# Token-major k of batch 0 by TensorE transposes, weights in 4 KB rows, two loads of constants and a first table laid anew

## The chip, the cores and the metric

One core of a Trainium2 chip runs the kernel. The metric is the device time of one execution in microseconds, lower is better. Three executions of the kernel before took 506.74, 506.96 and 507.01 us; the median, 506.96 us, is the time that counts.

## The reference, cut to what is computed

```python
def _attn_ref(q, k, v):                       # q, k, v: (8, 8, 576, 64): batch, head, position, feature
    scores = np.matmul(q, k.transpose(0, 1, 3, 2)) / np.sqrt(64)
    gamma = 1.0 - 2.0 ** (-5.0 - np.arange(8))
    rel = pos[:, None] - pos[None, :]
    Dmat = np.where(rel >= 0, gamma[:, None, None] ** rel, 0.0)
    return np.matmul(scores * Dmat, v)        # retention: causal, decaying with distance

def _moe_ref(x, w_in, w_spatial, b_spatial, w_out):   # x: (8, 576, 512), the heads side by side
    h = np.maximum(x @ w_in, 0.0)             # w_in 512 x 1024, float64
    u, v = h[..., :512], h[..., 512:]
    v_n = (v - v.mean(-1)) / np.sqrt(v.var(-1) + 1e-06)
    v_s = np.einsum('ts,bsd->btd', w_spatial, v_n) + b_spatial[None, :, None]
    return (u * v_s) @ w_out                  # w_out 512 x 512, float64
```

## The kernel before, in words

**Tiling.** Each of the 8 batches goes through a retention stage and then a gated stage. The 576 positions are four chunks of 128 and a tail of 64. Per chunk, retention needs q and k feature-major (`qk`, 128 partitions x 1024), v token-major (`vv`) and k token-major, scaled by a decay per head (`kn`). In the kernel before, `kn` is a second load of k from HBM, and `prep_k` scales it in place.

**Weights.** `w_in` and `w_out` arrive as 64-bit floats. `weight(kind, i)` turns one block into two fp32r parts, a high and a low one, in six steps over DVE, ACT, DVE, DVE, ACT and one more engine. Kind 1 is the v half of `w_in` (blocks of 128 rows, staged in `lent_slot`, parts in `win`), kind 0 its u half and kind 2 `w_out` (blocks of 128 columns, staged in `raw`). With the parts each product is three matmuls: high by high, high by low, low by high. Where matmuls of 512 columns write `m<-win,slot`, that is x times the v half; three of them are one group here.

**What sets the order.** Everything is written out by hand in tables of words. `run` walks a table and lets the named generator issue its next step, so each engine gets its instructions in the table's order and never passes one that waits. `ORDER` holds batches 0 and 1 whole and the retention of batch 2; `STEADY` follows four times and `LAST` ends it. `BANKS` names the PSUM bank of each product in turn. The words that matter here:

- `d.b.c` issues a load of chunk c of batch b on SP (SyncE's DMA queue); `D.kind.i` a block of weights; `c.a`, `c.t` constants; `T` a tail; `S` a part of `w_spatial`.
- `k.b.c` is `prep_k`, `q.b.c` is `prep_q` (q times a decay, tile `qsc`, on POOL).
- `g.b.c`: the scores of a chunk (`r<-qk`), then their mask on DVE (`at`).
- `p.b.c`: the update, k token-major times v (`r<-vv,kn`), then `sh`, decay, `st`, decay: the running state, on DVE and ACT (`dec`).
- `b.b.c`: the burst that ends a chunk: half of the carried products (`r<-qsc,sh`), a one-column copy on ACT (`r<-warm`), the other half, the values (`r<-at,vv`), and two evacuations, `slot` high on ACT and `slot` low on DVE.
- `v.b.s`: x times the v half for chunk s (4 the tail), then its norm. `t`, `e`: the tail. `U`, `V`, `G`, `P`, `y`, `X`, `F`: the later products of batches 0 and 1.
- `z.i.1`: one matmul of zeros, 128 x 512 (`m<-wsp`), that nobody reads. The table has 43 of them.

An instruction is named in the profile by the line of the helper that records it, L203, so the tiles tell them apart. Chunks of batch 0 wait in four places: chunks 0 and 1 in `qk`, `kn`, `vv`, chunk 2 in the tile `u`, chunk 3 in `lent_wout`.

## Time and profile before

| | |
|---|---|
| median of 3 executions | 506.96 us |
| the profiled execution | 506.91 us, of which the span from the first to the last instruction is 504.8 us |
| PE (TensorE matmul) busy | 498.3 us, 99% of the span |
| DVE, ACT, POOL busy | 389.2, 259.2, 152.5 us |
| DMA | 55.52 MB, 110 GB/s over the span |
| chain that ended last | PE 92%, DVE 4%, DMA 3%, ACT 1% |

Busy time of PE is modelled from its pipelined matmuls and says little where every slice is full; what a matmul takes is better read as the distance from one start to the next. The first 22 us are the only stretch in which the chain that ended last runs through DMA, ACT and DVE and not through PE.

### The profile page before, as it was taken

How to read it: one execution, taken by the hardware profiler on the slowest of the kernel's cores; microseconds unless marked ns; L12 is line 12 of the kernel's file. 1: busy time of each engine (PE TensorE's matmuls, PEld its weight loads, DVE VectorE, ACT ScalarE, POOL GpSimd, SP SyncE). 2: the span in 40 equal slices, each digit the busy share in tenths (PEclk: the TensorE clock that was granted, in tenths of full speed). 3: DMA queues.
4: the chain of work that ended last, by engine and by line, in shares of the span. 5: the costliest groups of instructions: out<-in, count | busy, mean ns of one | idle time of the engine just before them, and what ended most of it. 6: DMA issues, size and time to landing. Idle time of an engine off the chain costs nothing.

```text
span 504.8 us, 17011 instructions
## 1 busy us (share of the span) xinstructions
PE 498.3 (99%) x7335; PEld 472.8 (94%) x7335; DVE 389.2 (77%) x869; ACT 259.2 (51%) x587; POOL 152.5 (30%) x133
## 2 busy tenths in 40 slices
PE   8999999999999999999999999999999999999997
PEld 6688999999999999999999999999999999999997
DVE  3787798875899876888679786888867886788756
ACT  3788535654363642647236472446525574357513
POOL 1778733252137421335014250243303240020000
PEclk9999999999999999999999999999999999999999
DMA  8979340332426322153122442054221520011002
GB/s 283 410 260 316 113 142 3 96 112 95 121 65 189 127 66 84 57 176 94 63 79 92 150 141 80 6 162 148 72 86 41 186 91 3 1 36 59 1 2 94
DMA packets 29516, 55.52 MB, mean 110 GB/s; under 512 B 2945, under 2 KB 15361, under 8 KB 29186
## 3 DMA queue, kind: packets, MB, share of 16 engines
q1 hardware_dynamic: 29442, 54.45, 32.6%
q8 instruction: 57, 0.93, 0.8%
q14 instruction: 17, 0.14, 0.1%
HBM read 45.00 MB, written 9.44 MB: 108 GB/s over the span
## 4 chain that ended last, share of the span: by engine, by line
PE 92%; DVE 4%; DMA 3%; ACT 1%; issue 0%; SPq 0%
PE m L203 78%; PE r L203 13%; DVE u L203 2%; DMA lent_slot<-in_w_in 2%; DMA fixed_terms<-in_terms 1%; DVE slot L203 1%; ACT slot L203 1%; DVE lent_vn L203 0%; DVE m L203 0%; SPq L203 0%; DVE st L203 0%; DVE at L203 0%
## 5 line engine op out<-in xcount | busy, mean ns | idle before, releaser
L203 PE MATMUL m<-wsp,vn 128*128 128x288 f32 x768 | 113.8, 297 | 0.0
L203 PEld LDWEIGHTS m<-wsp,vn 128*128 128x128 f32 x768 | 105.7, 188 | 0.7
L203 DVE TENSOR_TENSOR u<-m,u 128x288 f32<-128x288 f32 (+1 forms) x132 | 57.2, 438 | 17.2 <-PE m L203 9.8
L203 ACT COPY u<-m 128x288 f32<-128x288 f32 (+1 forms) x92 | 34.6, 384 | 33.2 <-PE m L203 24.4
L203 PE MATMUL m<-slot,win 128*128 128x288 f32 x336 | 50.5, 296 | 0.0
L203 PEld LDWEIGHTS m<-slot,win 128*128 128x128 f32 x336 | 46.7, 188 | 0.8 <-ACT u L203 0.2
L203 DVE SCALAR_TENSOR_TENSOR u<-u,m 128x288 f32<-128x288 f32 x48 | 21.2, 451 | 25.3 <-PE m L203 25.1
L203 PE MATMUL m<-slot,wout 128*128 128x288 f32 x264 | 39.8, 296 | 0.0
L203 POOL TENSOR_TENSOR slot<-u,slot 128x576 fp32r<-128x576 f32 x7 | 10.0, 1432 | 93.2 <-ACT slot L203 93.2
L203 PEld LDWEIGHTS m<-slot,wout 128*128 128x128 f32 x264 | 36.5, 188 | 0.6 <-DVE vn L203 0.3
L203 PE MATMUL m<-win,slot 128*128 128x512 f32 (+1 forms) x168 | 37.0, 351 | 0.0
L203 ACT CAST slot<-u 128x576 fp32r<-128x576 f32 x32 | 21.5, 675 | 25.6 <-DVE u L203 25.4
L203 PEld LDWEIGHTS m<-win,slot 128*128 128x128 f32 x168 | 26.7, 188 | 4.7 <-DVE slot L203 0.4
L203 ACT CAST places<-u 128x576 fp32r<-128x576 f32 x21 | 14.2, 677 | 30.5 <-DVE u L203 30.3
L203 PE MATMUL m<-quarter,slot 128*128 128x256 f32 x216 | 29.7, 283 | 0.0
L203 ACT COPY r<-warm 1x2 f32<-1x2 f32 x32 | 4.9, 152 | 47.8 <-PE r L203 47.6
L203 DVE TENSOR_TENSOR at<-r,fixed_terms 128x512 f32<-128x512 f32 x32 | 21.9, 683 | 8.5 <-PE r L203 6.9
L203 POOL TENSOR_TENSOR kn<-kn,fixed_terms 128x512 f32<-128x512 f32 x15 | 16.1, 1075 | 39.3 <-DMA kn<-in_qkv 34.1
L203 POOL TENSOR_TENSOR places<-x,places 128x576 fp32r<-128x576 f32 x6 | 10.5, 1756 | 57.0 <-ACT places L203 55.3
L203 PE MATMUL m<-slot,part 128*128 128x288 f32 x168 | 27.3, 301 | 0.4
L203 PE MATMUL m<-wtl,vt 128*128 128x288 f32 (+1 forms) x128 | 27.4, 295 | 0.0
L203 PEld LDWEIGHTS m<-quarter,slot 128*128 128x128 f32 x216 | 26.9, 188 | 0.4
(164 smaller groups left out, 1214.4 us busy)
## 6 DMA issues: line engine op xcount, KB each, us to landing
qk<-in_qkv SPq DMA_DIRECT2D x30, 512.0 KB, 4.3
kn<-in_qkv SPq DMA_DIRECT2D x30, 256.0 KB, 4.8
vv<-in_qkv SPq DMA_DIRECT2D x30, 256.0 KB, 4.7
out<-u SPq DMA_DIRECT2D x28, 144.0 KB, 1.8
tail<-in_tails SPq DMA_DIRECT2D x8, 384.0 KB, 3.5
out<-o SPq DMA_DIRECT2D x18, 144.0 KB, 1.9
lent_slot<-in_w_in SPq DMA_DIRECT2D x4, 512.0 KB, 9.3
raw<-in_w_in SPq DMA_DIRECT2D x4, 512.0 KB, 11.2
```

The lines of the kernel that those rows point to most:

```text
L203: ins = op(*args, **kw)
```

## The change

Token-major k of the four chunks of batch 0 is no longer loaded. `prep_k` makes it with four TensorE transposes per chunk, from feature-major k and an identity (`eye`, 64 KB, a new load), into a PSUM bank, and the scaling then reads that bank and writes `kn`. `k.0.c` is therefore two steps in the table. In HBM the order of v and k token-major is exchanged, so that chunks 2 and 3 are one load of three quarters. The constants are cut in two: `fixed_terms` without the decay of q, and `qs`. The host lays the blocks of the u half and of `w_out` out so that each partition reads one row of 4 KB. The tail of `w_spatial` is stored twice, for one load where there were two. `ORDER` and `BANKS` are new throughout; `STEADY` and `LAST` are as before.

```diff
 ORDER = """
-    d.0.0 d.0.0 c.a q.0.0.p d.0.0 z.22.1 k.0.0.v z.4.1 z.0.1 z.12.1 z.26.1 z.36.1 z.27.1 z.17.1 z.18.1 z.29.1
...
+    d.0.0 z.32.1 z.5.1 z.12.1 z.21.1 c.e d.0.0 c.a z.29.1 z.25.1 z.31.1 z.8.1 z.6.1 z.10.1 z.4.1 z.28.1 z.18.1
...
-    fixed_terms = cp.tile([P, 2 * NP * D + NP * D + H + NP], F32, name="fixed_terms")
+    fixed_terms = cp.tile([P, 2 * NP * D + H + NP], F32, name="fixed_terms")
...
+    qs = cp.tile([P, NP, D], F32, name="qs")
...
+    def eye():
+        return keep("eye", [P, P], tag="o1")
...
-            parts = (qk, qkv[b, c, :, :2]), (kn, qkv[b, c, :, 2]), (vv, qkv[b, c, :, 3])
-        else:
-            parts = (t, qkv[b, c]),
+            parts = (qk, qkv[b, c, :, :2]), (kn, qkv[b, c, :, 3]), (vv, qkv[b, c, :, 2])
+            parts = parts if b else parts[::2]
+        else:
+            parts = (t[:, :3], qkv[b, c, :, :3]),
...
-            dma(t.bitcast(U64).rearrange("p (a n) -> p a n", a=NCB), w[:, i * P:(i + 1) * P].rearrange("(a p) n -> p a n", p=P))
+        dma(t.bitcast(U64), (w_u, w_v, w_out)[kind][i])
...
     def prep_k(b, c, eng=po):
         kh = chunk[b, c][2].rearrange("p (h d) -> p h d", h=H)
-        scale(kh, kh, kd, eng)
+        if b:
+            scale(kh, kh, kd, eng)
+            yield
+            return
+        ps = bank()
+        for p in range(NP):
+            pe.transpose(ps[:, p * P:(p + 1) * P], chunk[b, c][1][:, p], eye())
+        yield
+        scale(kh, ps.rearrange("p (h d) -> p h d", h=H), kd, eng)
+        yield
...
-        for i in range(2):
-            dma(w[i * TL:(i + 1) * TL, NC], w_sp[NC * P:, :])
+        dma(w[:, NC], w_sp[NC * P:, :])
```

On SP, at the start of the program, the loads stand like this before (`lent_slot` is a block of the v half):

```order
L203 DMA qk_94<-in_qkv 128x1024
L203 DMA kn_95<-in_qkv 128x512
L203 DMA fixed_terms<-in_terms 128x780
L203 DMA vv_96<-in_qkv 128x512
L203 DMA lent_slot_93<-in_w_in 128x512 x2
L203 DMA qk_171<-in_qkv 128x1024
L203 DMA kn_172<-in_qkv 128x512
L203 DMA vv_173<-in_qkv 128x512
L203 DMA lent_slot_93<-in_w_in 128x512 x2
L203 DMA u<-in_qkv 128x2048
L203 DMA raw<-in_w_in 128x4x128
```

and like this now, at the same place:

```order
L207 DMA qk_95<-in_qkv 128x1024
L207 DMA eye<-in_unit 128x128
L207 DMA vv_97<-in_qkv 128x512
L207 DMA fixed_terms<-in_terms 128x524
L207 DMA qk_121<-in_qkv 128x1024
L207 DMA lent_slot_94<-in_w_v 128x512
L207 DMA vv_123<-in_qkv 128x512
L207 DMA qs<-in_qterms 128x256
L207 DMA u<-in_qkv 128x1536
L207 DMA lent_slot_94<-in_w_v 128x512 x3
L207 DMA lent_wout_137<-in_qkv 128x1536
```

Chunks 2 and 3 stand earlier, three of the four blocks of the v half later, and `qs` is a load of its own.

On PE, from the first work after the fourteen leading matmuls of zeros to the values of chunk 0, before:

```order
L203 MATMUL r_91<-qk_94 64x64 x16
L203 MATMUL r_91<-vv_96,kn_95 64x64 x16
L203 MATMUL m_88<-wsp_68 128x512
L203 MATMUL r_90<-qsc_100,sh 64x64 x4
L203 MATMUL m_89<-wsp_68 128x512
L203 MATMUL m_86<-wsp_68 128x512
L203 MATMUL m_87<-wsp_68 128x512
L203 MATMUL m_86<-wsp_68 128x512
L203 MATMUL r_90<-qsc_100,sh 64x64 x4
L203 MATMUL r_90<-at_159,vv_96 64x64 x16
```

and now, from the same place, up to the transposes of chunk 1 (six matmuls of zeros follow there, then the rows of the next fence):

```order
L207 MATMUL m_89<-eye,qk_95 128x128 x4
L207 MATMUL m_90<-wsp_69 128x512
L207 MATMUL r_92<-qk_95 64x64 x16
L207 MATMUL r_92<-vv_97,kn_96 64x64 x16
L207 MATMUL m_87<-wsp_69 128x512
L207 MATMUL m_88<-wsp_69 128x512
L207 MATMUL m_89<-wsp_69 128x512
L207 MATMUL m_90<-eye,qk_121 128x128 x4
```

```order
L207 MATMUL r_92<-qk_121 64x64 x16
L207 MATMUL r_91<-qsc_128,sh 64x64 x4
L207 MATMUL r_92<-vv_123,kn_122 64x64 x16
L207 MATMUL r_91<-qsc_128,sh 64x64 x4
L207 MATMUL r_91<-at_195,vv_97 64x64 x16
L207 MATMUL m_89<-eye,u 128x128 x4
L207 MATMUL m_90<-wsp_69 128x512 x9
```

The scores and the update of chunk 1 now stand ahead of the values of chunk 0.

On ACT, from the evacuation of chunk 0 (`slot`) on, before (`u<-u` is the scaling of chunk 2's k, eight instructions):

```order
L203 CAST slot_207<-r_90 128x2x4x64
L203 CAST win_66<-lent_vn_92 128x512
L203 ACTIVATE dec_79<-sh,fixed_terms 128x64 x4
L203 COPY r_90<-warm 1x2
L203 CAST win_66<-lent_vn_92 128x512
L203 ACTIVATE m_87<-lent_slot_93 128x512
L203 ACTIVATE m_86<-lent_slot_93 128x512
L203 CAST slot_207<-r_90 128x2x4x64
L203 ACTIVATE u<-u,fixed_terms 128x64 x8
L203 CAST win_66<-lent_vn_92 128x512 x2
```

and now, up to the scaling of chunk 3's k (`lent_wout<-m`):

```order
L207 CAST slot_257<-r_91 128x2x4x64
L207 ACTIVATE dec_80<-sh,fixed_terms 128x64 x4
L207 ACTIVATE m_88<-lent_slot_94 128x512
L207 ACTIVATE u<-m_89,fixed_terms 128x64 x8
L207 ACTIVATE m_89<-lent_slot_94 128x512
L207 COPY r_91<-warm 1x2
L207 ACTIVATE dec_79<-st_76,fixed_terms 128x64 x4
L207 CAST win_67<-lent_vn_93 128x512 x3
L207 CAST slot_257<-r_91 128x2x4x64
L207 ACTIVATE m_87<-lent_slot_94 128x512
L207 ACTIVATE dec_80<-sh,fixed_terms 128x64 x4
L207 ACTIVATE lent_wout_137<-m_90,fixed_terms 128x64 x8
```

The scaling of chunks 2 and 3 stands earlier in ACT's list, the first `win` later.

## Rows read from the trace of the kernel before

**Rows 1.** The page, parts 1 and 2: busy time; busy tenths, granted clock.

```profile
PE 498.3 (99%) x7335; PEld 472.8 (94%) x7335; DVE 389.2 (77%) x869; ACT 259.2 (51%) x587; POOL 152.5 (30%) x133
...
PE   8999999999999999999999999999999999999997
...
PEclk9999999999999999999999999999999999999999
```

**Rows 2.** The chain that ended last, by time: start us, us, what.

```profile
1.64 5.37 DMA fixed_terms<-in_terms
...
7.02 10.73 DMA lent_slot<-in_w_in
...
17.77 0.35 DVE lent_vn L203
...
18.93 1.29 DVE m L203 x2
...
21.91 1.16 PE r L203 x64
```

**Rows 3.** The timeline of PE: start us, us, operation, out<-in, count.

```profile
1.50 6.32 PE L203 MATMUL m<-wsp 128*128 128x512 f32 x14 [1.50 <-DVE wsp L203]
...
7.75 0.69 PE L203 MATMUL r<-qk 64*64 64x64 f32 x32
8.27 0.65 PE L203 MATMUL r<-vv,kn 64*64 64x64 f32 x32
...
36.49 1.65 PE L203 MATMUL m<-win,slot 128*128 128x512 f32 x6
37.98 2.00 PE L203 MATMUL m<-win,xt 128*128 128x512 f32 x8
39.81 1.75 PE L203 MATMUL m<-slot,win 128*128 128x288 f32 x12
...
55.13 0.43 PE L203 MATMUL m<-wtl,vt 128*128 128x288 f32 x2
```

**Rows 4.** Groups of PE by form, 1.4 to 150 us: the zeros.

```profile
L203 PE MATMUL m<-wsp 128*128 128x512 f32 x43 | 15.3, 489 | 1.5 <-DVE wsp L203 1.5
```

**Rows 5.** Windows: busy PE, PEld, DVE, ACT, POOL; clock; DMA.

```profile
7.75:22.00 14.25, 12.93 (x272) 9.26 (x275) 9.96 (x20) 8.72 (x26) 8.32 (x7) 1.00 1.03 387
...
40.00:150.00 110.00, 110.00 (x1710) 103.72 (x1709) 87.40 (x186) 59.71 (x138) 44.65 (x38) 1.00 0.36 116
```

**Rows 6.** The timeline of ACT, with idle time before and its releaser.

```profile
11.25 0.66 ACT L203 ACTIVATE m<-lent_slot 128x512 f32<-128x512 f32 x1 [1.11 <-DMA lent_slot<-in_w_in]
...
19.88 0.59 ACT L203 CAST slot<-r 128x512 fp32r<-128x512 f32 x1 [1.24 <-PE r L203]
20.36 2.02 ACT L203 ACTIVATE u<-u,fixed_terms 128x64 f32<-128x64 f32 x8
22.29 1.13 ACT L203 CAST win<-lent_vn 128x512 fp32r<-128x512 f32 x2
23.32 1.07 ACT L203 ACTIVATE dec<-st,fixed_terms 128x64 f32<-128x64 f32 x4
24.28 0.62 ACT L203 ACTIVATE m<-raw 128x512 f32<-128x512 f32 x1
```

**Rows 7.** The timeline of DVE.

```profile
7.10 0.69 DVE L203 TENSOR_TENSOR kn<-kn,fixed_terms 128x512 f32<-128x512 f32 x1 [5.65 <-DMA fixed_terms<-in_terms]
...
12.44 0.70 DVE L203 SCALAR_TENSOR_TENSOR m<-m,lent_vn 128x512 int32<-128x512 int32 x1
13.04 0.68 DVE L203 SCALAR_TENSOR_TENSOR lent_vn<-lent_slot,m 128x512 int32<-128x512 int32 x1
```

**Rows 8.** The timeline of POOL.

```profile
7.14 1.24 POOL L203 TENSOR_TENSOR qsc<-qk,fixed_terms 128x256 f32<-128x256 f32 x1 [6.71 <-DMA fixed_terms<-in_terms]
13.56 1.05 POOL L203 TENSOR_TENSOR kn<-kn,fixed_terms 128x512 f32<-128x512 f32 x1 [5.18 <-DMA kn<-in_qkv]
...
22.97 2.57 POOL L203 TENSOR_TENSOR win<-lent_vn,win 128x512 fp32r<-128x512 f32 x2 [0.93 <-ACT win L203]
```

More of the change, by code (lines that the diff above doesn't have):

```diff
@@ new lines @@
+    p.0.0.va z.35.1 z.36.1 z.20.1 k.0.1.v z.27.1 z.1.1 z.42.1 z.2.1 z.17.1 z.3.1 p.0.0.va p.0.0.va p.0.0.va
+    p.0.0.va g.0.0 w.1.1.vp k.0.1.v g.0.1 b.0.0 p.0.1.aa b.0.0 w.1.1.vp b.0.0 b.0.0 b.0.0 p.0.1.aa w.1.1.vp
+    p.0.1.aa b.0.0 w.1.0.vp w.1.0.vp p.0.1.aa w.1.0.vp w.1.3.vp g.0.1 k.0.2.a k.0.2.a z.7.1 w.1.3.vp z.41.1 z.40.1
+    z.9.1 z.30.1 z.16.1 z.0.1 z.22.1 z.39.1 b.0.1 p.0.2.aa b.0.1 p.0.1.aa z.24.1 b.0.1 b.0.1 z.13.1 z.23.1 z.37.1
+    k.0.3.a g.0.2 w.1.1.vp w.1.0.vp w.1.3.vp w.1.3.vp w.1.0.vp w.1.1.vp q.0.2.p w.1.2.pp w.1.0.vp D.0.0 w.1.1.vp
@@ new lines @@
+    A.1.9.v A.1.2.p A.1.6.v A.1.12.p A.1.3 A.1.4.p F.0.1.0 F.0.1.0 v.1.4 k.2.1.a F.0.1.2 v.1.4 v.1.3 y.1.2.0
+    F.0.0.3 F.0.0.3 A.1.10 A.1.13.v F.0.1.3 A.2.0.p X.1.0.0 b.2.0 g.2.1 p.2.1.vv A.1.7 A.1.8.v A.2.1.v A.2.5.v
+    F.0.0.2 F.0.0.3 F.0.1.3 A.1.14 A.1.15.p p.2.0.vp F.0.1.2 y.1.2.0 b.2.0 b.2.0 b.2.0 X.1.0.0 A.2.2.v A.2.9.v
+    A.2.6.v q.2.1.v p.2.1.vv X.1.1.3 A.1.11.v A.2.12.v X.1.1.3 g.2.1 p.2.1.vv A.2.7 F.0.1.3 d.2.2 b.2.0 A.2.3
+    A.2.10 d.2.2 d.2.2 T.2 F.0.1.1 X.1.0.1 A.2.8.v p.2.1.vv X.1.0.1 A.2.13.v A.2.4.v y.1.0.1 y.1.1.1 X.1.1.2 t.2.v
@@ new lines @@
+    e.2.p Z.1.7.vv Z.1.6.vv k.3.0.v Y.1.2.v Z.1.4.vv W.1.2.0.A W.1.2.0.C W.1.2.1.A e.2.p Z.1.5.vv W.1.2.0.C
+    W.1.2.1.B W.1.2.0.B e.2.p b.2.3 Z.1.4.vv R.2.2.p W.1.2.0.A R.2.1.v W.1.2.1.A Z.1.4.vv R.2.1.v K.2.5.vp
+    W.1.2.0.A R.2.3.v W.1.2.1.A W.1.2.0.A W.1.2.1.A R.2.3.v W.1.2.1.B K.2.7.pv R.2.2.p W.1.2.0.E W.1.2.1.C
+    W.1.2.0.B g.3.0 W.1.2.0.E W.1.2.1.C d.3.1 d.3.0 d.3.1 W.1.2.1.B W.1.2.0.C d.3.1 W.1.2.1.B W.1.2.1.B W.1.2.0.B
+    K.2.6.vp K.2.4.vp W.1.2.0.B W.1.2.0.B p.3.0.pv p.3.0.pv p.3.0.pv q.3.0.p W.1.2.1.E p.3.0.pv p.3.0.pv W.1.2.1.E
@@ L92 @@
+    K.2.6.vp K.2.6.vp W.1.2.1.B K.2.7.pv W.1.2.1.E W.1.2.0.E W.1.2.0.B K.2.5.vp K.2.5.vp K.2.7.pv W.1.2.1.C
+    K.2.4.vp K.2.4.vp
 """
@@ L245, in load @@
             t = t.rearrange("p a n -> p (a n)")[:, :4 * 512].rearrange("p (a n) -> p a n", a=4)
[L246 removed]
+            qk, vv, kn = t[:, :2], t[:, 2], t[:, 3]
         else:
@@ L982, in _constants @@
     f = lambda a: np.ascontiguousarray(a, dtype=np.float32)
-    terms = np.concatenate([a.reshape(P, -1) for a in (am, qscale, kdec, per ** D)], axis=1)
-    return {"terms": f(terms), "tmask": f(amt)}
+    terms = np.concatenate([a.reshape(P, -1) for a in (am, kdec, per ** D)], axis=1)
+    return {"terms": f(terms), "qterms": f(qscale), "unit": f(np.eye(P)), "tmask": f(amt)}
 def _layout(q, k, v, moe_w_in, moe_w_spatial, moe_b_spatial, moe_w_out):
@@ L1007, in _layout, with cut @@
     c = np.ascontiguousarray
+    def cut(a):
+        return c(a.reshape(4, P, 4, P).transpose(2, 1, 0, 3).reshape(4, P, 512)).view(np.uint64)
+    w_in = moe_w_in.reshape(H, D, -1)[[0, 1, 3, 2, 4, 5, 7, 6]].reshape(H * D, -1)
+    w_sp = moe_w_spatial.T[:, _PLACES]
     return {
-        "qkv": c(np.stack([fc(qf), fc(kf), tkc(kn), tkc(vv)], axis=3)),
+        "qkv": c(np.stack([fc(qf), fc(kf), tkc(vv), tkc(kn)], axis=3)),
         "tails": c(np.stack([ends(qf), ends(kf), vt], axis=2)),
-        "w_in": c(moe_w_in.reshape(H, D, -1)[[0, 1, 3, 2, 4, 5, 7, 6]].reshape(H * D, -1)).view(np.uint64),
-        "w_sp": c(moe_w_spatial.T[:, _PLACES]),
+        "w_u": cut(w_in[:, :DH]),
+        "w_v": c(w_in[:, DH:]).view(np.uint64).reshape(NCB, P, DH),
+        "w_sp": c(np.concatenate([w_sp, w_sp[m:]])),
         "b_sp": c(moe_b_spatial.reshape(1, S)[:, _PLACES]),
-        "w_out": c(moe_w_out).view(np.uint64),
+        "w_out": cut(moe_w_out),
     }
```

94 lines of the change are left out of this document (37 added, 57 removed).

## The prediction

> **What bounds the kernel now.** I read the page first: PE is busy for 498.3 of 504.8 us and full in nearly every slice [rows 1]. Then the chain that ended last. Up to 21.91 us it runs through two loads and DVE: the constants until 7.01, the fourth block of the v half until 17.75, then DVE's work on that block [rows 2]. From 21.91 on it is PE's. The windows agree: between 7.75 and 22 PE is busy for 12.93 of 14.25 us, between 40 and 150 for 110.00 of 110.00 [rows 5]. The program after the first table is the same in both kernels, so the time moves by as much as PE's position in its work moves inside the first table. Three things can move it there: the matmuls of zeros, the new transposes, and PE's waits.
>
> The zeros don't change: 43 before [rows 4], 43 words now, and fourteen lead in both. These fourteen take 0.45 us each, from 1.50 to 7.75 [rows 3], twice what a matmul of 512 columns takes later (six from 36.49 to 37.98, 0.25 each [rows 3]), although the granted clock is shown at its upper level of 2.4 GHz in every slice [rows 1]. So the first real work starts at 7.75 as before, whatever has landed by then. The loads that are saved there can't start PE sooner; they only matter where a later instruction waits for one.
>
> **Prices.** Starts, not durations, count, because neighbours overlap. On PE: a 512-column matmul or a zero 0.24; the scores of a chunk 0.52 (7.75 to 8.27 [rows 3]), its update 0.55, its values 0.5, half of the carried products 0.15. On ACT: `slot` high 0.48, eight scalings of k 1.93, a `win` 0.52, four `dec` 0.96, `m` 0.6 (differences of the starts in [rows 6]). On DVE: `kn` 0.69, others of 512 columns 0.60 from start to start [rows 7], of 256 columns 0.42 as an estimate by their half size and a fixed part. On POOL: `qsc` of chunk 0 1.24, a `win` low 1.3 [rows 8].
>
> A transpose has no row. From below, a quarter of a zero: 0.06. From above, an ordinary product of this type: sixteen 64 x 64 ones, four side by side, take 0.52 [rows 3]; 128 x 128 fills the four places and has twice the columns, so 0.52 / 16 x 4 x 2 = 0.26. I take 0.12, half-way in ratio, as it lies nearer to the zeros, which also load fresh weights each time: 0.5 per chunk, 1.9 for all sixteen.
>
> Loads: by the bytes queued ahead of them, before: 1158 KB by 7.01 [rows 2], 2438 by 11.25 [rows 6], 3206 by 13.56 [rows 8], 4486 by 17.75 [rows 2], which is some 300 KB/us. The new queue has 2502 KB up to `qs`, so 11.4; chunk 2 is in at 13.7, the second, third and fourth v blocks at 15.4, 17.1 and 18.8. Chunk 3 stands at 5574 KB; 5510 KB were in by 20.36, when ACT scaled chunk 2 without a wait [rows 6], so 20.4.
>
> **The walk: chunk 0.** Transposes 7.75 to 8.25, a zero, scores to 9.0; DVE's `kn` from PSUM 8.4 to 9.1; update to 9.7. Before, the update was through by 8.9. ACT's `sh` 10.2, DVE's decay, `st`, mask and a step of a v block, then `kn` of chunk 1, ready at 12.75. PE meanwhile: three zeros, transposes of chunk 1 to 10.9, six zeros to 12.35, scores of chunk 1 to 12.85. The first carried half waits for `qsc`: `qs` 11.4 + 1.24 = 12.65, covered. Update 1 to 13.55, values 0 to 14.2. The load of `kn` that is gone held POOL until 13.56 before [rows 8], but now the transposes and the order put chunk 0's values 2.4 us later than before.
>
> **The walk: ACT.** From 14.3 ACT's list has no gap up to the scaling of chunk 3: `slot` 14.8, `dec` 15.75, `m` 16.35 (block in at 15.4), scaling of chunk 2 18.3, `m` 18.9, the one-column copy 19.0, `dec` 19.95, two `win` 20.97, the third when DVE's steps, held by the block of 17.1, are through, 21.65, `slot` of chunk 1 22.15, `m` 22.75, `dec` 23.7, scaling of chunk 3 25.7. The loads ahead of it would have to be over a microsecond late to show.
>
> **The walk: PE behind ACT.** Transposes of chunk 2 to 14.7, nine zeros to 16.85, a carried half; update 2 follows the scaling, 18.45 (a wait of 0.9); a zero, a half, values 1 to 19.7; three zeros, transposes of chunk 3 20.4 to 20.9; scores 2 21.45. The first groups of the v product need `slot` of chunk 1, high at 22.15 and low at 22.9 (`win` low, 20.45 + 1.3, is earlier): two groups by 23.85, a wait of 1.0. A half, scores 3, then update 3 behind the scaling at 25.75 (0.7); tail scores, half, values 2: 26.6. Eight groups (24 x 0.24) 32.4, two zeros 32.9, the burst of chunk 3, as long as before, 2.7: 35.6; six and twelve matmuls to 40.0, four zeros 40.95, eight of the tail 1.85: 42.8. Before, the tail's product was through at 39.81 [rows 3], with ten groups and six matmuls ahead of it; now it has four groups more ahead of it, 2.9 us. Like for like 39.9 against 39.81, and 0.1 more for one change between small and large matmuls that the walk leaves out: **0.2 us later**.
>
> **What hides at no cost.** The 4 KB rows, the single load for the tail of `w_spatial` and the shorter chunk loads end after 20 us, where PE waits for ACT, DVE or nothing; they are worth nothing, and if that cover were gone, 1 MB less at 300 KB/us would be worth 3.4 us. The later `qs` costs nothing up to 0.2 us of lateness, then one for one. The transposes of chunks 2 and 3 lie in waits of 0.9 and 1.0 us; uncovered they would cost 0.5 each. `kn` of chunk 1 moves from POOL to DVE, 0.69 us in a list that then waits for a load anyway. SP's list is past its loads of batch 0 before anything there waits.
>
> **The sum** is made against the profiled execution: 504.8 us of span and 2.1 around it, 506.9; the median is 506.96, so nothing is lost between them. 506.9 + 0.2 = **507.1 us**. With the ends of a transpose, 0.06 and 0.26, chunks 0 and 1 move values 0 by -0.4 and +1.1, which gives 506.7 and 508.0.
>
> The Trainium skill, on its page "TensorE: Matmul & The Clock Gate", section "Part 4: PE-mode transpose", speaks against the change: it measured about 275 ns for one transpose inside a kernel. By that figure sixteen are an estimated 4.4 us, those of chunks 0 and 1 some 1.2 us of them on the path, and the time about 508.1; no row here shows a transpose, and my 0.12 rests on the zeros alone.
>
> **Rivals.** *Faster: ACT's list is shorter than I sum it.* ACT reads k and the evacuations from PSUM where it read SBUF, and the waits of 0.9, 1.0 and 0.7 are what it holds. If values 0 are through by 13 or the list takes 10 instead of 11.4 us, PE waits some 1.5 us less: 505.6; with the groups of the v product starting at 21.5, 505.2. For it: between 7.75 and 22 ACT was busy for only 8.72 us [rows 5], so its order has slack to win. Against it: the new list has two scalings of 1.93 us ahead of what PE wants. It counts from 1.2 us on.
>
> *Slower: DVE behind on the norms.* The tail's norm must be through before the first product with the tail of `w_spatial`. That stood at 55.13 [rows 3]; now, by the order, PE gets there at about 51: 42.8, then 1.9 for a burst, 24 and 24 matmuls of 288 columns at 0.13 to 0.15. DVE has the same work for it in 4 us less. If it has more than 2.5 us too little, PE waits 1.5: 508.6. For it: DVE is busy for 87.40 of 110 us from 40 on, more than any engine but PE; against it: PE did not wait there [rows 5], and part of DVE's work moved ahead.
>
> *Transposes dear:* 0.26 each, 508.0, from 0.22 on at the edge of slower. *The change doing less than it says:* if the rounds of loads landed no sooner, only chunks 2 and 3 would be late; PE would then wait for chunk 3 after 20.4, one for one, 508; the sizes in the queue speak against it.
>
> **How the numbers follow.** A measurement of this kernel can tell about 0.2%, 1.0 us, from no change: 505.9 to 508.0. The forecast (507.1, own range 506.2 to 508.0) has 0.40; the faster rival 0.28; the slower one 0.18; dear transposes 0.10, half of them beyond 508.0; late chunk 3 0.04, as slower. Faster 0.28, same 0.45, slower 0.27. For 8 in 10 the range reaches into both rivals: 505.2 to 508.8.
>
> **What would show it.** In the profile of the changed kernel: the transposes at 7.75 and the distance of four of them (0.5); values of chunk 0 through at about 14.2; ACT without a gap from 14.3 to 25.7; update 3 ending near 25.8; the product of the tail starting near 41 after 18 matmuls and four zeros; PE without a wait from 43 on. The prediction is wrong if ACT has gaps there, if a transpose is above 0.2 or if PE waits for DVE between 43 and 60.

## The result: 510.7 us, 0.8% slower, and the profile after

The changed kernel takes 510.7 us (median; 510.61 to 511.17) against 507.0 for the kernel before, a ratio of 1.0078 with a 95% interval of 1.0064 to 1.0092. The forecast was 507.1, range 505.2 to 508.8: the direction (no change) and the range were both wrong. The profiled execution spans 508.5 us against 504.8.

The page of the changed kernel, answering to [rows 1]: PE differs in its first three slices (of 12.7 us each), 7, 8 and 7 tenths where it had 8, 9 and 9 before; the gap told of below lies in the third.

```profile
span 508.5 us, 17047 instructions
...
PE 497.7 (98%) x7351; PEld 473.6 (93%) x7351; DVE 392.8 (77%) x870; ACT 258.8 (51%) x587; POOL 151.1 (30%) x132
...
PE   7879999999999999999999999999999999999997
...
PEclk9999999999999999999999999999999999999999
```

PE's waits between 1 and 43 us (who waited for what: us in total, times, the longest); from 43 to 160 us PE waits for nothing:

```profile
PE r L207 <- issue: 2.8, 1, 2.8
PE m L207 <- DVE wsp L207: 1.5, 1, 1.5
PE r L207 <- DVE kn L207: 1.1, 1, 1.1
PE r L207 <- ACT u L207: 0.8, 1, 0.8
PE m L207 <- DVE slot L207: 0.6, 1, 0.6
PE r L207 <- POOL qsc L207: 0.4, 1, 0.4
```

The largest is "issue": PE stood, and waited for nothing that the profile knows. The chain that ended last has this gap on the path (start us, us, what):

```profile
12.64 0.72 POOL qsc L207
...
15.12 0.59 ACT slot L207
...
17.13 1.74 ACT u L207 x8
...
25.39 1.97 PE r L207 x112
27.36 2.82 issue
30.18 0.69 PE r L207 x29
```

PE's timeline, answering to [rows 3] (start us, us, operation, count, idle before):

```profile
1.50 5.10 PE L207 MATMUL m<-wsp 128*128 128x512 f32 x14 [1.50 <-DVE wsp L207]
6.44 0.60 PE L207 MATMUL m<-eye,qk 128*128 128x128 f32 x4
...
8.97 0.69 PE L207 MATMUL r<-vv,kn 64*64 64x64 f32 x32 [1.07 <-DVE kn L207]
...
19.00 0.69 PE L207 MATMUL r<-u 64*64 64x64 f32 x32 [0.82 <-ACT u L207]
...
27.14 0.22 PE L207 MATMUL r<-qsc,sh 64*64 64x64 f32 x1
30.18 0.69 PE L207 MATMUL r<-at,u 64*64 64x64 f32 x32 [2.82 <-issue]
30.80 5.80 PE L207 MATMUL m<-win,slot 128*128 128x512 f32 x24
...
44.87 1.99 PE L207 MATMUL m<-win,xt 128*128 128x512 f32 x8
```

From start to start the gap ahead of the values of chunk 2 is 3.0 us. Their operands had long been there: the mask (`at`) was done at 24.75, v had landed at 14.35, and the weight load of the first of them ran at 27.13.

**The account.** The tail's product starts at 44.87. Before, it started at 37.98 [rows 3], with twelve matmuls of the v product fewer ahead of it; here 24 of them take 5.64 us from start to start, so twelve are 2.82. Like for like the tail's product is 4.07 us later. From its start to the end of the span it is 463.7 us here, 464.0 before (466.8 less the 2.8), and 463.2 to 464.7 in every kernel below with the new table; so what is late there is late at the end. Of the 4.07 us, 3.0 are the gap, and about 1 is the front. POOL's `qsc` waited for its factors `qs` until 12.48, 1.1 us after their forecast, and PE waited for `qsc` until 13.41. DVE's `kn` waited for the constants until 8.12, but it started at 8.22, where the forecast had 8.4.

```profile
8.22 0.69 DVE L207 TENSOR_TENSOR kn<-m,fixed_terms 128x512 f32<-128x512 f32 x1 [6.77 <-DMA fixed_terms<-in_terms]
```

```profile
15.12 0.59 ACT L207 CAST slot<-r 128x512 fp32r<-128x512 f32 x1 [0.48 <-PE r L207]
...
17.13 1.73 ACT L207 ACTIVATE u<-m,fixed_terms 128x64 f32<-128x64 f32 x8
...
24.56 1.72 ACT L207 ACTIVATE lent_wout<-m,fixed_terms 128x64 f32<-128x64 f32 x8
...
31.00 0.59 ACT L207 CAST slot<-r 128x512 fp32r<-128x512 f32 x1 [2.54 <-PE r L207]
```

ACT's list (the rows above, answering to [rows 6]) is 0.6 to 0.8 us later than its forecast, and then idle for 2.54 us behind PE's gap.

**What the gap is.** One thing in the gap is not a load of the program: a packet on the queue that the profile calls "instruction". In the trace's DMA records it runs from 27.79 to 28.67 us. The DMA view from 22.6 to 27.7 us has no such packet (first line), the one from 27.7 to 28.8 has one:

```profile
q1 hardware_dynamic: 484, 1.43, 92.7%
...
q1 hardware_dynamic: 167, 0.38, 98.6%
q8 instruction: 1, 0.02, 5.0%
```

The span has 57 of them, 16 KB each. PE has 14,776 entries in the trace (weight loads, matmuls and PE's own semaphore entries), which is 259 for each packet. That suggests that PE had run through the instructions it held; this document calls that a dry run. The Trainium skill, page "Runtime: NRT & Kernel Launch", section "Instruction fetch mechanics", says that an engine's instructions are refilled in blocks of 16 KiB, 256 instructions, at a cost that is "mostly hidden". The trace agrees on the block; on the cost it differs here, and the experiments say by how much.

### The profile page after: what moved, and what is told of

Its sections match the earlier page's. It is cut to its first block, busy times and chain, and to the rows that moved or that the text cites. A ratio compares the mean times of both kernels' runs of the same rounds, so it can differ in the third digit from the quotient of the medians.

```text
span 508.5 us, 17047 instructions
## 1 busy us (share of the span) xinstructions
PE 497.7 (98%) x7351; PEld 473.6 (93%) x7351; DVE 392.8 (77%) x870; ACT 258.8 (51%) x587; POOL 151.1 (30%) x132
## 4 chain that ended last, share of the span: by engine, by line
PE 89%; DVE 4%; DMA 2%; issue 1%; ACT 1%; POOL 1%; SPq 1%; POOLq 0%; DVEq 0%; ACTq 0%
PE m L207 76%; PE r L207 13%; DVE u L207 2%; DMA u<-in_qkv 2%; DVE slot L207 1%; SPq L207 1%; ACT slot L207 1%; DVE kn L207 0%; POOL x L207 0%; ACT u L207 0%; POOL places L207 0%; POOL dec L207 0%; ACT dec L207 0%; DVE places L207 0%; DVE x L207 0%
## 5 line engine op out<-in xcount | busy, mean ns | idle before, releaser
L207 PE MATMUL m<-wsp,vn 128*128 128x288 f32 x768 | 112.6, 296 | 0.0
L207 PE MATMUL m<-win,slot 128*128 128x512 f32 (+1 forms) x168 | 35.0, 348 | 0.6 <-DVE slot L207 0.6
L207 POOL TENSOR_TENSOR qk<-qk,qs 128x512 f32<-128x512 f32 (+1 forms) x16 | 20.4, 1273 | 21.5 <-PE r L207 21.5
L207 PE MATMUL m<-places,wout 128*128 128x288 f32 x168 | 26.7, 298 | 0.0
## 6 DMA issues: line engine op xcount, KB each, us to landing
qk<-in_qkv SPq DMA_DIRECT2D x30, 512.0 KB, 4.1
lent_slot<-in_w_v SPq DMA_DIRECT2D x4, 512.0 KB, 9.7
raw<-in_w_u SPq DMA_DIRECT2D x4, 512.0 KB, 6.5
```

The costliest lines, as they stand in the source:

```text
L207: ins = op(*args, **kw)
```

## Experiments 1: what PE waits for

An entry's number below is its place in the order of PE's starts. Entry 961 is the last ahead of the gap: 476 weight loads, 475 matmuls and ten semaphore and drain entries. A trace is one execution, and executions of one kernel below spread over 1 to 6 us. The trace shows where PE stands; what a change costs is read from the median and its interval, always as a ratio to the kernel before.

**quarters.** The fourteen leading zeros are cut in four: 42 more matmuls at the head, the same columns.

```diff
...
         for i in range(n):
-            pe.matmul(ps, idle[:, :P], idle, start=True, stop=True)
+            for j in range(4 if led else 1):      # led: one of the first fourteen
+                cut = slice(j * P, (j + 1) * P) if led else slice(0, 512)
+                pe.matmul(ps[:, cut], idle[:, :P], idle[:, cut], start=True, stop=True)
```

> The changed kernel, its fourteen leading zero matmuls each cut into four of 128 columns: the same columns, 42 more matmuls, so 84 more TensorE records (each matmul leaves one of weight load and one of matmul) ahead of everything else; nothing else differs. In the changed kernel TensorE stands from 27.14 to 30.18 us with nothing that the profile waits for, after its 961st record, and a packet of the instruction queue of 16 KB is on its way from 27.79 to 28.67; 57 such packets for 14,776 records are 259 records each. Theory A, TensorE had run out of fetched instructions: the run dry comes 84 records earlier in the work (after record 877 of the old count, at about 26.5), the packet is asked for 84 records earlier too, where TensorE stands in slow matmuls (record 684, at 22.4 instead of 25.7), and so it lands in time: the gap shrinks from 3.0 to under 0.5 us, and the time falls from 510.7 to about 507.9. Theory B, a wait at that place in the work for something that the profile doesn't name (a buffer, a load): the gap stays at 3.0 ahead of the values of chunk 2, 510.7. Theory C, the loss is spread over the front (constants and chunk 2 landing later) and the gap only takes up slack: gap gone, but the time stays within 0.5 of 510.7.

Measured: 519.5 us, ratio 1.0251 (1.0202 to 1.0300). My premise failed: the quarters took 12.0 us where the whole ones took 4.9, so the front is 7 us late. The time therefore says nothing of the theories, but the place of the gap does. The one ahead of chunk 2's values is gone, and a new one stands in other work, 3.0 us from start to start:

```profile
34.20 0.65 PE L207 MATMUL r<-at,u 64*64 64x64 f32 x32
...
46.42 0.34 PE L207 MATMUL r<-att,tail 64*64 64x64 f32 x5 [2.75 <-issue]
```

That is behind entry 1473, which is 961 + 2 x 256. Theory B, a wait that belongs to the work, falls here.

**products_first.** Two groups of the v product go ahead of the scores of chunk 3.

```diff
-... w.1.2.pp v.0.1 v.0.0 k.0.3.a t.0.p b.0.2 g.0.3 ...   m k.1.0.p v.0.1 v.0.1 v.0.0 v.0.0 ...
+... w.1.2.pp v.0.1 v.0.0 v.0.1 v.0.0 k.0.3.a t.0.p b.0.2 g.0.3 ...   m k.1.0.p v.0.1 v.0.0 ...
```

> The changed kernel with two groups of three v products (the second of two chains) put ahead of the scores and update of chunk 3 instead of behind the values of chunk 2. TensorE waits 0.4 us there for ScalarE's scaling, and 1.4 us of products fit in. Theory A (TensorE ran out of fetched instructions at record 961): 12 slow records more lie between the request for the packet and the run dry, so the gap shrinks by about 1.4 of its 3.0 us and its place moves 12 records earlier in the work, into the second half of the carried part: 510.7 - 1.4 to 1.8 = about 509.1. Theory B (an unnamed wait ahead of the values of chunk 2): the place stays ahead of the values, they begin at 30.2 as before, and the 1.4 us of products are gained all the same: 509.3. The place of the gap tells A from B here, the time doesn't. Theory C (the loss is the late front): under 0.5 gained.

Measured: 509.6, ratio 1.0048 (1.0032 to 1.0064). The gap is 1.6 us instead of 3.0 and has moved twelve entries back in the work, into the carried half, as theory A (PE had run out of instructions) says. This is the only kernel with the new table whose whole interval lies no higher than the lower end of the changed kernel's (1.0064):

```profile
29.39 0.21 PE L207 MATMUL r<-qsc,sh 64*64 64x64 f32 x1 [1.34 <-issue]
```

**terms_first.** The constants and the factors `qs` go earlier on the load queue.

```diff
-    ... c.e d.0.0 c.a ...   k.0.0.v d.0.1 D.1.1 d.0.1 c.q q.0.0.p
+    ... c.e c.a d.0.0 ...   k.0.0.v d.0.1 c.q D.1.1 d.0.1 q.0.0.p
```

> The changed kernel with two loads moved on the load queue alone: the 262 KB of decay constants ahead of v of chunk 0, and the scaling of q ahead of the v weights' second block. In the changed kernel VectorE's scaling of k of chunk 0 waits for the constants until 8.12 us, and the q scaling of chunk 1 waits for its factors until 12.48; both were forecast about 1.1 earlier. Theory C (the late front is the loss): update of chunk 0 at 8.2 instead of 8.97, values 0 at about 14.0 instead of 14.95, and most of that 1 us is kept: 509.7. Theory A or B: TensorE stands behind ScalarE from 17 us on whatever the front does, the values of chunk 0 come earlier, but the scaled chunk 2 doesn't, so under 0.3 us is kept, 510.4 to 510.9, with a gap of 3 us again near 27 to 30.

Measured: 509.4, ratio 1.0052 (1.0032 to 1.0072). The new order of loads moved the front's lateness from one load to another. Chunk 0's `kn` began at 7.40 instead of 8.22 and the carried half no longer waited for `qsc` (13.02 instead of 13.41). But the block of the v half now lands behind `qs`; DVE stood 0.67 us for it, and `kn` of chunk 1 began at 13.20 instead of 11.94. So the values of chunk 0 were through 0.3 us later, at 15.26, and update 2, behind ACT's scaling, came at 19.31 instead of 19.00. The gap is 2.8 us and the tail's product starts at 44.90, as in the changed kernel. This doesn't test theory C (the loss is the late front), since the front stayed late. The median lies nearer to C's 509.7 than to the 510.4 to 510.9 of A and B, but its interval overlaps the changed kernel's and the traced execution is the slowest of the four (510.66). What the front alone costs stays open.

**forty_more.** Forty small zero matmuls go where PE waits for the constants.

```diff
-    k.0.0.v z.38.1 g.0.0 p.0.0.va
+    k.0.0.v g.0.0 z.38.1 p.0.0.va       # z.38: 40 zero matmuls of 64x64 go behind it
```

> The changed kernel with 40 small zero matmuls (64x64, four records each: 160 more TensorE records) put where TensorE waits 1.3 us for the decay constants, between the scores and the update of chunk 0; one zero matmul goes behind the scores with them. No work is left out and no wait is taken away. In three kernels so far the gap stood right behind record 961, whichever work stood there, and in the one with 84 more records it stood behind record 1473, which is 961 + 2 x 256. Theory A (supply in pieces of 256 records): record 961 is now the work that was record 801 (26.0 us), and its packet is asked for 160 records earlier in the work, at 19.6 instead of 22.6 us; the gap shrinks from 3.0 to at most 1.2 us, and the next pieces begin in slow matmuls: 507.7 to 509.0. Theory B (a wait of the work itself): gap of 3.0 ahead of the values of chunk 2 as before, 510.7 or more.

Measured: 513.3, ratio 1.0118 (1.0101 to 1.0135). The time missed its forecast: the forty took 4.6 us, not the 1.3 that were free, so the update of chunk 0 is over 4 us late. Yet the values of chunk 2 start at 30.88, only 0.7 later than in the changed kernel: the gap is gone. Two others came, 0.9 us behind entry 1217 and 1.4 behind entry 1473, both 961 plus a multiple of 256.

**loaded_k** and **fewer_zeros** take entries away ahead of the gap.

```diff
-        for p in range(NP):
-            pe.transpose(ps[:, p * P:(p + 1) * P], chunk[b, c][1][:, p], eye())
         yield
-        scale(kh, ps.rearrange("p (h d) -> p h d", h=H), kd, eng)
+        scale(kh, kh, kd, eng)              # loaded_k: kn is loaded again
```

```diff
-z.27.1 z.1.1 z.42.1 z.2.1 z.17.1 z.3.1   ...   z.41.1 z.40.1 z.9.1 z.30.1 z.16.1 z.0.1     # fewer_zeros
```

> The changed kernel with the transposes undone: token-major k of batch 0 is loaded again (1 MB more in the first 26 us, the identity's 64 KB less) and scaled where it lies; table, rows and constants as in the changed kernel. 32 TensorE records fewer lie ahead of 27 us, so record 961 falls in the middle of the values of chunk 2. Theory A: the dry run stays, 2 to 3 us, and moves by 32 records; chunks 2 and 3 land 1.3 to 2.6 us later, which costs up to 2 us more: 510.5 to 513. Theory T (the transposes make the loss): 507 to 508.5 and no gap.

> The changed kernel without 12 of the zero matmuls that fill TensorE's waits between 9 and 18 us: 24 records fewer, no work left out. Record 705 now falls right behind TensorE's wait of 0.9 us for VectorE's half of the states (old record 729, at about 24.2 us) instead of 22 records ahead of it. Theory A with the request held up by TensorE's own wait (in three kernels the packet came 3.4 to 3.75 us after the end of that wait): packet at 27.5 to 28, the dry run 24 records later in the work, in the middle of the values of chunk 2, 2.7 to 3.0 us long: 510 to 511. Theory A with a request at record 705 and a slow transfer of 5.2 us: packet at 29.4, gap 4.5: 512. Theory Z (the zeros themselves delay the work): the values of chunk 2 begin over 1 us earlier, under 509.7.

Measured: loaded_k 512.0, ratio 1.0098 (1.0073 to 1.0124); fewer_zeros 512.3, ratio 1.0111 (1.0091 to 1.0131). With 32 entries fewer the gap stands after 16 of the 32 matmuls of those values, with 24 fewer after 12. So theory T (the transposes make the loss) falls: without them the gap is still there, and 2 us longer. In fewer_zeros PE also stood 1.3 us behind entry 449.

```profile
26.48 0.44 PE L207 MATMUL r<-at,u 64*64 64x64 f32 x16
31.65 0.70 PE L207 MATMUL r<-at,u 64*64 64x64 f32 x16 [4.73 <-issue]
```

```profile
27.40 0.41 PE L206 MATMUL r<-at,u 64*64 64x64 f32 x12
30.80 0.56 PE L206 MATMUL r<-at,u 64*64 64x64 f32 x20 [3.00 <-issue]
```

The count ahead of the gap is the same in all of them. Windows from 0 to a time inside the gap, of the changed kernel, terms_first, products_first, loaded_k and fewer_zeros (the x behind PE and PEld are the matmuls and weight loads so far):

```profile
0.00:28.00 28.00, 23.00 (x475) 17.91 (x476) 14.17 (x29) 16.09 (x52) 9.20 (x12) 1.00 0.87 305
```

```profile
0.00:28.00 28.00, 23.44 (x475) 18.08 (x476) 14.66 (x29) 15.74 (x51) 8.96 (x12) 1.00 0.88 304
```

```profile
0.00:28.50 28.50, 24.79 (x475) 19.30 (x476) 14.13 (x29) 16.12 (x52) 9.19 (x12) 1.00 0.90 314
```

```profile
0.00:29.00 29.00, 22.36 (x475) 17.11 (x476) 15.72 (x31) 16.91 (x53) 10.76 (x13) 1.00 0.95 352
```

```profile
0.00:29.00 29.00, 22.00 (x475) 16.91 (x476) 14.94 (x31) 16.53 (x53) 10.00 (x13) 1.00 0.85 302
```

Whatever work stands there, PE stops behind its 475th matmul. And it goes on 1.3 to 1.5 us after the packet's end in each: 28.67 and 30.18 in the changed kernel, 28.08 and 29.39 in products_first, 28.73 and 30.21 in terms_first, 30.34 and 31.65 in loaded_k, 29.49 and 30.80 in fewer_zeros; 45.06 and 46.42 in quarters. So PE's instructions come in pieces of 256; a piece that PE runs through before the next has landed costs the rest of the wait. This is shown. What is not shown is a kernel that loses the gap and with it the time. Where the gap at entry 961 is gone, another dry run or another wait has come (forty_more above, the held loads below). That 3.0 of the 4.07 us are the gap rests on the timeline, and on products_first.

Why here: in the changed kernel entries 706 to 961 took 4.55 us (22.59 to 27.14), in the kernel before 5.83 (23.59 to 29.42), because zeros and groups of the v product stood between the small matmuls of chunks 2 and 3. And the packet came 5.2 us after entry 705, where before it came 2.8 us after it (at 26.35) and landed 2.1 us ahead of need. The kernel before, from 23.6 to 26.3 us (first line) and from 26.3 to 27.4:

```profile
q1 hardware_dynamic: 620, 1.07, 102.9%
...
q1 hardware_dynamic: 250, 0.42, 99.6%
q8 instruction: 1, 0.02, 5.5%
```

With a packet 2.8 us behind entry 705, 1.0 us long, and PE going on 1.4 us after it, the values of chunk 2 would have started at about 27.8. By this estimate 2.4 of the 3.0 us are the late packet, and 0.6 the closer matmuls.

## Experiments 2: why the packet is late

**sp_later.** One load, the first block of `w_spatial`, goes behind others.

```diff
-... p.0.3.ap S D.0.1 d.1.1 c.t ... d.1.0 S S S d.1.1 ...
+... p.0.3.ap D.0.1 d.1.1 c.t ... d.1.0 S S S S d.1.1 ...
```

> The changed kernel with one load put later on the load queue: the first 288 KB block of the spatial weights, whose destination comes free at 20.1 us and which holds back every load behind it from 12.5 to 20.1, goes behind the loads of batch 1's first chunk, next to its three sisters. Theory A (TensorE ran out of fetched instructions; the packet asked for at record 705, 22.6 us, came only at 27.8 because the loads that had been held back were all under way at once): the held-back loads run from 13 to 24 us, the packet comes 2.5 to 3.1 us after record 705 as in the kernel before, and the gap of 3.0 us at record 961 shrinks to 0 to 0.6: 507.6 to 508.3. Theory A2 (the run dry is only a matter of how fast TensorE goes through these 256 records, 4.5 us against 5.8 before): the gap stays above 2 us, 510 to 510.7.

Measured: 511.6, ratio 1.0086 (1.0071 to 1.0101). A miss: the loads ran on at 390 to 420 GB/s, and the packets came 5.4 and 5.9 us after entries 449 and 705. Now PE ran dry twice, for 2.5 us behind 705 and 1.4 behind 961.

**held** and **held_products** (the second on products_first): GpSimd writes one column of a buffer, so that the load into it, and all behind it on the queue, must wait.

```diff
+    def hold():
+        po.memset(keep("qk1", [P, 2, 512])[:, :, :1], 0.0)
+        yield
...
-... S D.0.1 d.1.1 c.t ...
+... S D.0.1 h d.1.1 c.t ...
```

> The changed kernel with the loads behind the second u block held back on the load queue: GpSimd clears one column of q and k's buffer of batch 1's second chunk behind its scaling of the tail, at about 24.5 us, and that chunk's load, the next on the queue, has to wait for it (21.4 to 24.5); everything behind it moves as much. The packet of instructions that TensorE lacks at 27.1 us is asked for behind record 705, between 22.6 and 25.7 us. Theory L (it is late because the loads crowd it): with only 288 KB and 512 KB under way it comes within 1 us of the request, by 26 us, and the gap falls under 0.5: 507.6 to 508.6, if the loads of batch 1, 3 us later, are not waited for. Theory R (it is asked for late, since the request waits behind TensorE's own waits for VectorE and ScalarE, which end at 24.2 and 25.7): it comes at 26.5 to 27, the gap falls to 1 to 2 us. Theory N (neither, its time is fixed by the work before): 27.8, gap 3.0, 510.7.

> The same hold of the loads, with the two groups of three v products ahead of chunk 3's scores as in the earlier run of these products, in which the gap was 1.6 us. Theory L: no gap, and the products in TensorE's wait bring 0.7 us: 506.6 to 508.0. Theory R: gap under 0.5, 507 to 508.3. Theory N: gap of 1.6, 509.5.

Measured: held 511.1, ratio 1.0085 (1.0059 to 1.0110); held_products 509.8, ratio 1.0053 (1.0036 to 1.0071). Both times miss theory L's forecast (L: the loads crowd the packet out), and so do those of the next four kernels. The packet is as L says: with the next loads issued from 24.78 us on instead of 21.75, it came 2.2 and 2.3 us after entry 705 instead of 5.2. Theory R (it is asked for only behind PE's own waits) forecast 26.5 to 27. In held it came at 25.07, ahead of the scores of chunk 3 at 26.01, for which PE waits for ACT; in held_swapped_products below it came at 23.48, ahead of the end of PE's wait for DVE (23.79) too. So R falls. In held the values of chunk 2 start at 27.71 instead of 30.18, with 0.3 us of the gap left. But the held loads are late for batch 1:

```profile
35.98 0.27 PE L207 MATMUL r<-qsc,sh 64*64 64x64 f32 x1 [1.37 <-POOL qsc L207]
...
38.19 0.88 PE L207 MATMUL r<-vv,kn 64*64 64x64 f32 x32 [1.64 <-POOL kn L207]
```

POOL waits 4.12 us for batch 1's q and k ahead of the first. More than the 2.5 us is given back: the tail's product starts at 47.07, 2.2 us later than in the changed kernel. The granted clock was at its lower level for part of that stretch, 0.55 on average from 38.2 to 42 us.

**held_early** and **early_unheld** (both on held_products): q and k of batch 1's first chunk go ahead.

```diff
-... S D.0.1 h d.1.1 c.t ... d.1.0 ...
+... d.1.0 S D.0.1 h d.1.1 c.t ...        # early_unheld: the same without h
```

> As the held loads with the v products ahead of chunk 3's scores, and one load taken out of the hold: q and k of batch 1's first chunk, for which GpSimd waited 4.1 us there and TensorE 0.9 and 1.3 us behind it (33 to 36 us), go ahead of the spatial weights' first block, where the load queue stands from 12 to 20 us. Theory L (the loads crowd out the packet; what the hold gave was given back at those waits): no gap at record 961, no waits of over 0.6 us at 33 to 36: 506.6 to 507.9, so the changed kernel without the stall comes within 0.2% of the kernel before. Rival (the front of the changed kernel is itself 2 us late behind ScalarE, whatever the packet does): 508.0 to 509.5.

> The same order of loads and products, without the hold: the loads of batch 1 come as soon as the queue lets them. Theory L: the packet behind record 705 is crowded out again, 4.5 us or more, gap of 1 to 1.6 at record 961: 508 to 509.3. If the hold costs more than it gives: under the time of the held one.

Measured: held_early 510.5, ratio 1.0062 (1.0045 to 1.0078); early_unheld 510.7, ratio 1.0074 (1.0058 to 1.0090). No forecast of either time held. The early load fills the stretch ahead, and the dry runs move to an earlier mark: in held_early the packets come 5.4 and 5.7 us after entries 449 and 705, and PE stands 1.1 us behind 449 and 2.0 behind 705; in early_unheld 1.2 behind 705 and 1.0 behind 961.

**held_swapped** and **held_swapped_products** (the second with the groups of the v product ahead): batch 1's first chunk goes first behind the hold.

```diff
-... S D.0.1 h d.1.1 c.t ... d.1.0 ...    # h on qk1
+... S D.0.1 h d.1.0 c.t ... d.1.1 ...    # h on qk0
```

> The held loads once more, with q and k of batch 1's first chunk (waited for by GpSimd there, 4.1 us) first behind the hold, and those of its second chunk third; the hold is on the first chunk's buffer. Theory L (the stall alone makes the loss): the packet behind record 705 comes within 3 us, no gap over 0.5 at record 961, and the waits of 1.8 and 1.9 us at 34 to 38 us go: span 510.3 - 3.6 = 506.7, so 508.0 to 508.6, 0.3% above the kernel before, the rest being the late front (1.1 us at the values of chunk 2). Rival: another wait takes the place of these, 509.5 or more.

> The same with the two groups of v products ahead of chunk 3's scores. Theory L: no gap, no waits at 33 to 36; the span of the held loads with products, 509.2, less the waits of 0.9, 1.3 and 0.6 us: 506.4, so 507.6 to 508.3. Rival: another wait takes their place, 509.5 or more.

Measured: held_swapped 511.7, ratio 1.0096 (1.0083 to 1.0109); held_swapped_products 510.5, ratio 1.0074 (1.0056 to 1.0091). In held_swapped no gap of over 0.2 us is left at entry 961 and the values of chunk 2 start at 27.36, but the load behind the swapped one is now the late one:

```profile
36.67 0.99 PE L207 MATMUL r<-vv,kn 64*64 64x64 f32 x32 [1.91 <-DMA vv<-in_qkv]
```

The rival holds: another wait took the place. In held_swapped_products PE stood 0.9 us behind entry 449 and 0.9 behind entry 705, because the packets came 3.9 us after entries 193 and 449; its tail's product starts at 43.84, the earliest with the new table, where 40.8 would be as early as before. The queue has little slack: in the kernel before, the loads run without a pause to 32 us, and here those that were held for some 3 us were waited for.

What follows: holding loads back brings the packet 3 us earlier (2.1 to 2.3 us in four kernels against 4.9 to 5.7 in terms_first, products_first and early_unheld). The volume alone is not the measure: in kernels with the old order the packets came 2.2 to 3.9 us after such an entry with the loads at 380 to 420 GB/s, in sp_later 5.4 and 5.9 at the same rate. What about the order of the loads makes the difference stays open. So does the moment at which a packet is asked for, which the trace does not show.

## Experiments 3: the parts of the change

**rows_alone**: the kernel before with `w_u` and `w_out` laid out by `cut` and nothing else.

```diff
-            w = w_in if kind == 0 else w_out
-            dma(t.bitcast(U64).rearrange("p (a n) -> p a n", a=NCB), w[:, i * P:(i + 1) * P].rearrange("(a p) n -> p a n", p=P))
+        dma(t.bitcast(U64), (w_u, w_v, w_out)[kind][i])
```

> The kernel before with one part of the change alone: the u and out weights laid so that a load's rows are 4 KB instead of 512-column pieces; order, table and everything else of before. Forecast of the prediction's step on rows: worth nothing, 506.8 to 507.2, since no wait of the kernel before that lies on its end is for a weight's load. Rival: the loads behind them land earlier and the wait of ScalarE for the v weights (11.25 us) shortens: up to 0.5 us faster.

Measured: 506.5, ratio 0.9992 (0.9981 to 1.0003). Worth nothing within 0.2%, as forecast.

**transposes_alone** and **old_table**: the parts on the table of the kernel before.

```diff
-    d.0.0 d.0.0 c.a q.0.0.p d.0.0 z.22.1 k.0.0.v
+    d.0.0 c.e c.a d.0.0 q.0.0.p z.22.1 k.0.0.v k.0.0.v      # old_table: c.q ahead of q.0.0.p
```

> The kernel before, its own table, with one part of the change alone: token-major k of batch 0 from TensorE transposes, each with its scaling right behind it (chunk 1's on VectorE instead of GpSimd), the identity loaded behind the first q and k, and the four loads of token-major k gone (1 MB of the first 26 us). Weights, constants and order as before. Theory A (the loss of the changed kernel comes from the new table, which brings small matmuls closer together and holds back the load queue): the transposes add 1.6 us of TensorE work, mostly beside waits, and the loads behind land 0.6 us earlier per chunk; no gap of over 1 us behind record 193 + 256 n: 505.3 to 507.6. Theory T (transposes themselves cost what the changed kernel lost): 509 or more.

> All parts of the change (transposes, 4 KB rows, two loads of constants, one tail load of the spatial weights) on the table and the order of the kernel before, in which only the loads that fall away are left out, the new ones put in, and each transpose stands right ahead of its scaling. Theory A (the loss is the new table's): 505.2 to 507.5, and no gap of over 1 us behind record 193 + 256 n. Theory T (the loss is in the parts): 509 or more, as the changed kernel.

Measured: 517.7, ratio 1.0208 (1.0178 to 1.0239), and 517.8, ratio 1.0235 (1.0191 to 1.0279). Neither tells what the parts cost: behind the first zero, PE waited for the identity until 5.3 and 5.2 us with thirteen zeros queued behind it.

**old_order** and **old_order_2**: all parts, the transposes put where their operand has landed.

```diff
-... z.18.1 z.29.1 ...   z.2.1 z.30.1 ... k.0.1.p g.0.1 ...   b.0.1 b.0.1 z.24.1 ... k.0.2.a
+... z.18.1 k.0.0.v k.0.0.v z.29.1 ...   z.2.1 k.0.1.v z.30.1 k.0.1.v ... g.0.1 ...   b.0.1 k.0.2.a b.0.1 z.24.1 ... k.0.2.a
```

> All parts of the change (transposes, 4 KB rows, constants in two loads, one tail load) in the order of the kernel before, this time with the transposes where their operand has landed and ahead of the work that needs them: chunk 0's behind the ninth of the fourteen leading zeros instead of behind the first (behind the first, TensorE waited for the identity until 5.2 us with the other zeros queued behind it, and the scores of chunk 0 began 3.1 to 3.7 us later than before), chunk 1's among the zeros ahead of its scores, chunk 2's ahead of the values of chunk 1, chunk 3's ahead of its scores; five zeros stand ahead of a transpose instead of behind it. Theory A (the parts cost nothing, the loss is the new table's closer small matmuls): packets of the instruction queue come 2.2 to 3.7 us after record 193 + 256 n in this order, no gap over 1 us there; the loads land up to 3 us earlier than before, ScalarE's chain from 14 to 26 us shortens a little: 505.0 to 507.0. Theory T (the parts cost by themselves): 508.5 or more.

> As the kernel with all parts of the change in the order of the kernel before, with two steps put right: VectorE's scaling of chunk 1's k stood ahead of two products of v weights and waited 1.19 us for the transposes; it goes behind them. Chunk 3's transposes stood behind the values of chunk 2, and ScalarE's scaling waited 1.00 us for them; they go ahead of those values, and three zero matmuls back to where they stood before. Theory A (the parts cost nothing where they are not waited for): the update of chunk 1 follows its scores at about 15.1 us instead of 17.3, the v weights' later blocks land at 14.6 and 15.9 instead of 16.5 and 17.8, so that VectorE's wait of 1.9 us for them goes, and the values of chunk 1 begin at 18 to 19 us: 505.0 to 507.0. Theory T (the parts cost by themselves): over 508.

Measured: 511.0, ratio 1.0071 (1.0052 to 1.0090), and 512.2, ratio 1.0116 (1.0094 to 1.0137). Neither has a gap of over 0.25 us right behind an entry 193 + 256 n ahead of 90 us, so the dry run belongs to the new table. But both are slower, and both have a wait that my placing made. In old_order DVE's `kn` of chunk 1 waited 1.2 us for the transposes, and PE then 1.6 us for DVE's `sh` ahead of the carried products of chunk 1 (17.29 instead of 15.99 before). In old_order_2 chunk 3's transposes hold a PSUM bank that a v product needs until ACT has scaled (1.7 us). The granted clock was at its lower level behind either wait. Whether that is all of their loss is not shown: what the parts cost when well placed in the old order was not found.

## Why the prediction was wrong, step by step

- **The step that failed** is the walk of PE behind ACT. It adds durations and waits for other engines, and has no term for PE's own instructions. Values 2 were to be through at 26.6 and were through at 30.80: 4.2 us, of which 3.0 are the dry run and the rest the late front. Behind them the walk holds: 16.2 us forecast to the end of the tail's product, 16.0 measured. Of the signs that the prediction named, a transpose above 0.2 and a wait for DVE behind 43 us did not come, and ACT's gaps up to 25.7 were 0.5 us at most. The sign that did was the tail's product, at 44.87 instead of near 41.
- **The loads** were mis-sized at the start, by up to 1.3 us: the 300 KB/us came from landings of before, and the first ones run slower (constants in at 8.12, where 1094 KB at that rate give 6.8; `qs` at 12.48 against 11.4, chunk 2 at 14.35 against 13.7). Those behind were right (v blocks 15.57, 16.80, 18.29; chunk 3 20.18 against 20.4). Update 0 still came as forecast (through at 9.59 against 9.7); values 0 were 0.8 us late and update 2 1.2.
- **The zeros**: the fourteen were to end at 7.75 and ended at 6.44, and between 6.17 and 7.64 in the kernels above that lead with whole ones. The prediction wondered that they are so slow with the clock at its upper level. The page of the profile misled it: the trace's record of the granted clock begins at 7.67 us in the kernel before and at 5.00 in the changed one, and the page counts the time ahead of the record as full. Here the zeros start some 0.43 us apart up to 5.07 and 0.23 behind it; before, all are 0.43 apart. In loaded_k matmuls of 512 columns start 0.43 apart where the record shows the lower level of 1.2 GHz (32.9 to 37.6 us) and 0.23 where it shows the upper. So the leading zeros ran at the lower level, and their end varies with the moment at which the clock rises. Nothing was won by the 1.3 us, since `kn` waited for the constants.
- **The transposes** were right: 0.089 us each from start to start for chunks 0 and 1 (four from 6.44 to 6.80), 0.10 and 0.13 for the others, against 0.12. The prediction's prices for dear ones slipped: 0.26 each adds 1.1 to 507.1, which is 508.2 and not 508.0. Nothing measured hangs on it.

```profile
L207 PE MATMUL m<-eye,qk x8: 270/272/273, 6.4 to 10.7; 128*128 128x128 f32 x8
```

  The Trainium skill's 275 ns ("TensorE: Matmul & The Clock Gate", section "Part 4: PE-mode transpose") is what the trace shows for the duration of one; its distance from the next is a third of that, so the estimate of 4.4 us for sixteen was too high. The time that the prediction put beside it, 508.1, should by its own sum (507.1 and 1.2) have been 508.3.
- **ACT's list** ended its scaling of chunk 3 at 26.28, forecast 25.7; its gap before that (0.40 us for DVE) is small. Update 3 ended at 26.71, forecast 25.75.
- **Rivals**: DVE behind on the norms did not happen (PE waits for nothing from 43 to 160 us), transposes were not dear, chunk 3 was not late, and ACT's list was not shorter. None of them was the dry run. Half of it was to be seen in the kernel before: a packet of that queue 2.8 us behind entry 705, and 2.1 us of slack, of which closer small matmuls use up 1.3. That the packet would come 5.2 us behind was not to be seen there.

## What to carry to other kernels

Count TensorE's entries (two a matmul in this trace) and put marks every 256. In these kernels PE could go on behind a mark only after the packet's delay (counted from the mark before), the packet's length of about 1.0 us and some 1.3 us more. With delays of 2.2 to 3.9 us that is 4.5 to 6.2 us, with 4.9 to 5.9 it is 7.2 to 8.2. PE runs dry when it is through a piece of 256 in less. Small fp32 matmuls gathered in one place were the danger here; long matmuls between them hid the fetch. A wait put down to "issue" with no releaser is read with the instruction queue's packets beside it.
